# FFN, query and output projections of an attention + FFN block as four 32-column tiles

## The chip, the cores and the metric

The kernel runs on one core of a Trainium2 chip. The metric is the device time of one execution in microseconds (us); "before" is the median of three runs. A core has five engines that run their own instruction streams and wait for each other by semaphores: TensorE (PE; it multiplies, its weight loads are shown apart as PEld), VectorE (DVE), ScalarE (ACT), GpSimd (POOL) and SyncE (SP, which here issues most transfers). Products land in PSUM, eight banks of 128 partitions by 512 fp32 columns; everything else lies in SBUF.

## The reference

One block, attention with one shared key and value head beside an FFN, both on the same normalised input:

```python
xn = _layernorm(x)                       # x: 1 x 2048 x 640
# A: 32 query heads of 20 columns, one key head and one value head
q = (xn @ wq).reshape(B, S, 32, 20).transpose(0, 2, 1, 3)
k, v = xn @ wk, xn @ wv                  # 2048 x 20 each
scores = einsum("bhqd,bkd->bhqk", q, k) * 20 ** -0.5
o = einsum("bhqk,bkd->bhqd", softmax(scores), v)
A = o.transpose(0, 2, 1, 3).reshape(B, S, 640) @ wo
# B: FFN, 640 -> 1728 -> 640
Bf = silu(xn @ w1) @ w2
out = x + A + Bf
```

All inputs and the output are bf16.

## The kernel before

**Units and steps.** A unit is one head on one chunk of 512 queries: 32 heads by 4 chunks, 128 units. Three units form a group, and a group runs over 16 tiles of 128 keys, one *step* each: 43 groups, 688 steps. In a step `do_S` computes the scores of the group's units (L776): three matmuls of 32 rows by 128 columns, which stand in different row strips of the PE array and run together. Two sets of three PSUM banks (0 to 2, 3 to 5) take turns. ScalarE takes the exponential of two units at once (L794, 1,024 columns) into a ring E of `NBLK` blocks of 512 columns in SBUF. The third unit's exponential is worked out on VectorE (L808, L878) and GpSimd (L814) by integer arithmetic, in 637 of the 688 steps; in the others ScalarE takes three (1,536 columns).

**Sums with V.** `pv_mm` (L866) multiplies the exponentials by V: 128 rows by 32 columns. Each unit has a column strip of its own, so that three or four such matmuls run side by side, all into PSUM bank 6. After a group's last step VectorE copies the sums out, a transposing transfer turns them, GpSimd and VectorE divide by the sum of weights, and the result goes into o.

**Projections ("jobs").** A `Job` is a list of matmuls into one PSUM bank with a `consume` step after it. In the loop over steps all jobs share bank 7. `qd_job` makes queries (L1064, 5 matmuls of 512 columns, for 128 or, in one piece, 96 output columns of wq); `h_job` makes an FFN hidden tile (L1100, 5 of 512, then tanh on ScalarE L1113 and a product on VectorE L1118). The 14th hidden tile has 64 columns: `pair` puts two chunks of it into the two halves of one bank (L1103, 64-column tiles). `out_job` makes half an output row tile (320 columns): 14 FFN matmuls (L1168, the last on 64 rows only) or 5 of the output projection (L1173); `hold_job` (L1231, L1236) does this for the last rows and keeps the bank. All of these use the whole array, 128 by 128. So do the transposes (L1548), the key (L1567) and value (L1587) projections and the first query job (L1039) of the start.

**Order.** Nothing waits for a queue decision on the chip: `Sched` plays the program through with assumed durations and writes each engine's instructions in the resulting order. For PE, `step` chooses: scores first when they can start; else sums with V ("PV") or a job ("M"). It stays with the kind that PE is in (`pe_mode`), goes to PV under `press` (more than `NBLK - PV_PRESS` blocks of the ring waiting), and otherwise prefers PV if two are ready. `switch` adds `SWITCH` to the assumed duration when the kind changes. Jobs are taken from a queue in order, not before their `min_step`, which `fill_chunk` spreads over a chunk's steps; the last 16 steps prefer PV. Where PE has nothing to do, `fill` issues matmuls on zeros (L693, L699, L712) that change no result, if PE's recent share of work is low.

**The start.** x is loaded, statistics are taken, tiles are normalised into w2's space (`xa`), and transposed by PE or by transposing transfers (L1517). `late_loads` then loads w2 (L1353) and wo, and GpSimd doubles wo (L1539).

Of the kernel before, what the change touches and what calls it, by code (L numbers as in the profile page):

```python
# [14 lines left out]
P = 128  # L15
D = 640
H = 32
# [28 lines left out]
NBLK = 31  # L46
# [38 lines left out]
ACT_STATS = (4, 6, 9, 12, 14)  # L85
NW_ENG = ("dve", "dve", "dve")
# [258 lines left out]
class Job:  # L345
    def __init__(self, name, mms, reads, consume, gate=None, min_step=-1, banks=None, on_start=None, width=0, hold=None, use=None, n=1):
        self.name = name
        self.mms = mms
# [12 lines left out]
class Builder:  # L361
# [17 lines left out]
    def alloc(self):  # L379
# [4 lines left out]
        self.w2 = sb([P, FC, D], BF16)  # L384
# [186 lines left out]
    def step(self, now):  # L571
# [44 lines left out]
        if pv_n and (self.pe_mode == "PV" or press or self.pv_q[0].mode == "M"):  # L616
# [14 lines left out]
        if choice == "PV":  # L631
            head = self.pv_q[0]
            d = (0.216 if head.mode == "PV" else head.dur) + self.switch(head.mode)
        else:
            d = (job if job is not None else cand[0]).mms[0][0] + self.switch("M")
# [39 lines left out]
    def fill(self, now, until):  # L675
# [4 lines left out]
        onto = job is not None and job.begun and job.width > 0 and (self.pe_mode == "M" or not self.u_open)  # L680
        mode = "PV" if self.u_open and not onto else "M"
# [5 lines left out]
        if onto:  # L687
# [4 lines left out]
            def fn(pe):  # L692
                return pe.matmul(self.bk(b, 0, n), self.zero[:, 0:P], self.zero[:, 0:n], start=False, stop=False,  # L693
# [7 lines left out]
        else:  # L701
# [8 lines left out]

            def fn(pe):
                return pe.matmul(self.bk(b, 0, n), self.zero[:, 0:P], self.zero[:, 0:n], start=True, stop=True)  # L712
# [3 lines left out]
        op = sc.new("pe", n / 2400.0 + self.switch(mode), fn, [("zero",)], [ukey] if ukey else [],  # L716
# [16 lines left out]
    def do_mm(self, job, now, d):  # L733
# [6 lines left out]
        self.pe_mode = "M"  # L740
# [124 lines left out]
    def pv_mm(self, pe, q, w, kt, x, start, stop):  # L865
        return pe.matmul(self.bk(UBANK, 0, QW, q * SLOT, (q + 1) * SLOT), self.v[:, w, kt, :], x, start=start, stop=stop,  # L866
                         tile_position=(0, q * SLOT), skip_group_check=True)

# [188 lines left out]
    def qd_job(self, c, m, step=-1):  # L1057
# [4 lines left out]
        for k in range(DC):  # L1062
            def f(pe, b, k=k):
                return pe.matmul(self.bk(b, 0, QW, 0, rows), self.wq[:, k, lo:hi], self.xnT[:, k, c * QW:(c + 1) * QW],  # L1064
                                 start=(k == 0), stop=(k == DC - 1))
# [24 lines left out]
        return Job(f"q{c}_{m}", mms, reads, consume, min_step=step, width=QW if rows == P else 0)  # L1090

    def h_job(self, c, fk, step):
# [4 lines left out]
        for k in range(DC):  # L1097
            def f(pe, b, k=k):
                if not pair:
                    return pe.matmul(self.bk(b), self.w1[:, k, fk * P:(fk + 1) * P], self.xnT[:, k, c * QW:(c + 1) * QW],  # L1100
                                     start=(k == 0), stop=(k == DC - 1))
                for z in range(2):
# [577 lines left out]
```

## Time and profile before

| | |
|---|---|
| median of three runs | 734.33 us (733.43 to 734.65) |
| span of the profiled execution | 732.1 us |
| granted TensorE clock, mean | 0.997 |
| exponentials on ScalarE, L794 | 688 instructions, 661.9 us busy |
| scores on PE, L776 | 2,048 matmuls |
| sums with V on PE, L866 | 3,534 matmuls |
| projections on PE, L1064, L1100, L1168, L1173 | 95, 260, 448 and 144 matmuls |
| fills on PE, L693, L699, L712 | 5, 47 and 70 matmuls |

The span runs from the first to the last instruction of the profiled execution; a run's time holds some us more. A row of the profile gives line, engine, operation, tiles and shape, with the count behind an x; behind that come busy time and mean duration (ns) of one, and behind a further bar the idle time ahead of them with what ended it. In a timeline the first two numbers are start and length in us. A matmul's record lasts from its start until its results are out (about 0.38 us for 512 columns), and the next starts while it is still running; the distance of starts is what a piece costs the engine.

### The profile page before, as it was taken

The page shows a single profiled execution, that of the slowest core. Times are in us where ns is not written, and L with a number is a line of the kernel's source. Part 1 is how long each engine was busy: PE and PEld are TensorE (multiplying, and loading weights), DVE is VectorE, ACT ScalarE, POOL GpSimd, SP SyncE. Part 2 cuts the span into 40 slices and gives each one's busy share as a digit, 9 for nine tenths or more (in the row PEclk, how much of TensorE's full clock was granted, in tenths as well). Part 3 has the DMA queues.
Part 4 walks back from the last instruction along what each step waited for, and adds up shares of the span by engine and source line. Part 5 has one row for each costly group of instructions (what it writes and reads, how often), then busy time and mean ns, then how long its engine had stood idle before and what let it go on. Part 6 is the DMA issues. An engine that isn't in the chain of part 4 may idle for free.

```text
span 732.1 us, 18886 instructions
## 1 busy us (share of the span) xinstructions
PE 714.9 (98%) x6863; PEld 229.2 (31%) x6863; DVE 652.6 (89%) x1189; ACT 695.8 (95%) x780; POOL 524.8 (72%) x897
## 2 busy tenths in 40 slices
PE   8898999999999999999999999999999999999998
PEld 4432222223333233222333233222233322322335
DVE  7788898998998999999899999999989899999883
ACT  6999999999999999999999999999999999999960
POOL 4376877677787777777777777767778877776770
PEclk9999999999999999999999999999999999999999
DMA  9546000000003011000102011110002001200011
GB/s 273 148 123 190 15 17 17 21 15 17 23 9 44 9 52 52 21 18 17 9 8 52 9 26 46 40 19 23 14 8 45 9 9 34 62 9 8 9 38 37
DMA packets 58546, 29.22 MB, mean 40 GB/s; under 512 B 44406, under 2 KB 57814, under 8 KB 58454
## 3 DMA queue, kind: packets, MB, share of 16 engines
q1 hardware_dynamic: 56998, 27.79, 15.1%
q8 instruction: 56, 0.92, 0.6%
q10 hardware_dynamic: 1456, 0.22, 0.2%
q14 instruction: 36, 0.29, 0.1%
HBM read 11.44 MB, written 2.62 MB: 19 GB/s over the span
## 4 chain that ended last, share of the span: by engine, by line
PE 70%; ACT 20%; issue 5%; DVE 4%; DMA 1%; POOL 1%; DVEq 0%; ACTq 0%; POOLq 0%
PE psall L866 23%; PE psall L776 22%; ACT sbt L794 18%; PE psall L1168 8%; PE psall L1100 7%; PE psall L1173 2%; PE psall L1064 2%; PE psall L712 2%; ACT sbt L1113 1%; DVE sbt L808 1%; PE psall L699 1%; DMA sbt<-sbt 1%; DVE sbt L1118 1%; ACT sbt L1458 1%; DVE sbt L1438 0%
## 5 line engine op out<-in xcount | busy, mean ns | idle before, releaser
L794 ACT ACTIVATE sbt<-psall 128x1024 bf16<-128x1024 f32 (+2 forms) x688 | 661.9, 1110 | 9.2 <-PE psall L776 7.7
L814 POOL TENSOR_TENSOR sbt<-sbt 128x256 int32<-128x256 int32 x637 | 436.8, 692 | 158.6 <-DVE sbt L808 143.9
L808 DVE TENSOR_SCALAR sbt<-psall 128x512 int16<-128x512 f32 x637 | 425.9, 684 | 48.2 <-PE psall L776 43.3
L776 PE MATMUL psall<-sbt 32*128 32x512 bf16 x2048 | 269.6, 385 | 6.4 <-ACT sbt L794 3.3
L866 PE MATMUL psall<-sbt 128*32 128x512 bf16 x3534 | 269.2, 385 | 2.1 <-POOL sbt L814 2.1
L776 PEld LDWEIGHTS psall<-sbt 32*128 32x128 bf16 x2048 | 69.2, 91 | 246.8 <-ACT sbt L794 81.1
L878 DVE TENSOR_SCALAR sbt<-sbt 128x1536 int16<-128x1536 int16 (+1 forms) x218 | 132.0, 608 | 2.0
L866 PEld LDWEIGHTS psall<-sbt 128*32 128x32 bf16 x3534 | 66.8, 94 | 113.7 <-issue 77.6
L1168 PE MATMUL psall<-sbt 128*128 128x320 bf16 x448 | 85.4, 302 | 0.2 <-DVE sbt L1118 0.2
L1100 PE MATMUL psall<-sbt 128*128 128x512 bf16 x260 | 79.9, 384 | 2.2 <-DVE sbt L1118 1.9
L1168 PEld LDWEIGHTS psall<-sbt 128*128 128x128 bf16 x448 | 34.7, 97 | 43.7 <-issue 33.1
L1118 DVE SCALAR_TENSOR_TENSOR sbt<-sbt,psall 128x512 bf16<-128x512 bf16 x54 | 36.8, 682 | 2.3 <-ACT sbt L1113 0.7
L1113 ACT ACTIVATE sbt<-psall 128x512 bf16<-128x512 f32 x54 | 37.1, 687 | 0.0
L986 DVE CAST sbt<-psall 128x512 bf16<-128x512 f32 x43 | 29.3, 682 | 1.7 <-PE psall L866 1.6
L1100 PEld LDWEIGHTS psall<-sbt 128*128 128x128 bf16 x260 | 17.8, 97 | 40.7 <-issue 25.8
L1064 PE MATMUL psall<-sbt 128*128 128x512 bf16 (+1 forms) x95 | 29.2, 385 | 0.4 <-DVE sbt L1118 0.4
L1173 PE MATMUL psall<-sbt 128*128 128x320 bf16 x144 | 29.0, 303 | 0.5 <-issue 0.4
L972 POOL TENSOR_TENSOR sbt<-sbt 128x240 bf16<-128x240 f32 (+2 forms) x44 | 25.4, 578 | 2.3 <-DMA sbt<-sbt 1.4
L958 POOL TENSOR_TENSOR sbt<-sbt 128x44 f32<-128x44 f32 x84 | 26.0, 309 | 1.1
L956 POOL CAST sbt<-sbt 128x168 f32<-128x168 bf16 x42 | 14.1, 335 | 9.0 <-DMA sbt<-sbt 9.0
L712 PE MATMUL psall<-sbt 128*128 128x512 bf16 (+1 forms) x70 | 17.4, 403 | 1.9 <-POOL sbt L1368 1.5
L1185 DVE SCALAR_TENSOR_TENSOR sbt<-psall,sbt 128x320 bf16<-128x320 f32 x28 | 13.6, 486 | 6.1 <-PE psall L1168 5.9
(88 smaller groups left out, 207.9 us busy)
## 6 DMA issues: line engine op xcount, KB each, us to landing
sbt<-in_A_x_dram SPq DMA_DIRECT2D x32, 160.0 KB, 3.3
out_dram<-sbt SPq DMA_DIRECT2D x15, 160.0 KB, 1.8
sbt<-in_B_w_dram SPq DMA_DIRECT2D x5, 432.0 KB, 6.6
sbt<-sbt SPq DMA_DIRECT2D x105, 20.0 KB
sbt<-in_B_w_dram SPq DMA_DIRECT2D x13, 160.0 KB, 2.9
sbt<-sbt SPq DMA_TRANSPOSE x68, 2.4
sbt<-sbt SPq DMA_DIRECT2D x1, 1024.0 KB, 6.1
sbt<-in_A_wo_dram SPq DMA_DIRECT2D x5, 160.0 KB, 2.7
```

The lines of the kernel that those rows point to most:

```text
L776: ins = pe.matmul(self.bk(par3 + j), self.kT[r:r + SLOT, kk, kt * P:(kt + 1) * P], self.qT[r:r + SLOT, h // 4, (x // H) % 2, :], start=Tru ...
L794: return a.activation(self.E[:, b0 * QW:(b0 + na) * QW], self.ps[:, par3 * BANK:(par3 + na) * BANK], AF.Exp, scale=ACT_SCALE)
L808: return v.tensor_scalar(self.Z[:, zs, zp * QW:(zp + 1) * QW], self.bk(bb), 0.0, ZMAX, ALU.max, ALU.min)
L814: sc.new("pool", Y_TIME, lambda v: v.tensor_tensor(self.Y[:, zs, 1, zp * QW:(zp + 1) * QW].bitcast(I32), self.Z[:, zs, zp * QW:(zp + 1) * ...
L866: return pe.matmul(self.bk(UBANK, 0, QW, q * SLOT, (q + 1) * SLOT), self.v[:, w, kt, :], x, start=start, stop=stop, tile_position=(0, q * ...
L878: sc.new("dve", Y_SLOW + t_dve_4x(w), lambda v, k=k: v.tensor_scalar(self.Y[:, zs, k, 0:n * QW], Z, float(PH[k + 1][0]), None, ALU.add), z ...
L1064: return pe.matmul(self.bk(b, 0, QW, 0, rows), self.wq[:, k, lo:hi], self.xnT[:, k, c * QW:(c + 1) * QW], start=(k == 0), stop=(k == DC - 1))
L1100: return pe.matmul(self.bk(b), self.w1[:, k, fk * P:(fk + 1) * P], self.xnT[:, k, c * QW:(c + 1) * QW], start=(k == 0), stop=(k == DC - 1))
L1113: sc.new("act", t_act(QW), lambda a: a.activation(t, src, AF.Tanh, scale=0.5), [("B", b)], [("tb", tp)], prio=X_PRIO, name=f"th{c}_{fk}")
L1118: sc.new("dve", t_dve_ps(QW), lambda v: v.scalar_tensor_tensor(out=self.hT[0:rows, fk, :], in0=t, scalar=1.0, in1=src, op0=ALU.add, op1=AL ...
L1168: return pe.matmul(self.bk(b, 0, 320), self.hT[r0:r1, fk, i * P:(i + 1) * P], self.w2[r0:r1, fk, e0:e0 + 320], start=(m == 0), stop=(m == ...
L1173: return pe.matmul(self.bk(b, 0, 320), self.oT[:, k, i * P:(i + 1) * P], self.wo[:, k, e0:e0 + 320], start=(m == 0 and src != "ps"), stop= ...
```

## The change

The jobs of `qd_job`, `h_job`, `out_job` and `hold_job` issue each matmul as four (for 96 columns three) matmuls of 128 rows by 32 columns, side by side, as the sums with V do (`mm4`). Their `mode` is now "PV", so for the planner no change of kind lies between them and the sums with V; the first query job, keys, values and transposes keep "M". When such a job is ready and there is no `press`, `step` takes it ahead of the sums with V. The last FFN tile is used with all 128 rows: w2 gets a 15th slice, and GpSimd zeroes the 14th and 15th (after their last use as normalised x, before w2 is loaded), so that for each chunk the other half of the rows meets zero weights. For the space, the ring E has 30 blocks in place of 31. The fills at the start get shapes from a list, `WARM` (M: 128 by 128; T: four of 128 by 32; H: two of 128 by 64; S: three of 32 by 128; A: twelve of 32 by 32), and the first nine are assumed to last twice as long.

```diff
-NBLK = 31
+NBLK = 30
+WARM = "MMMMMMMMMMMMMAATTATMMAMSSASTMMHTHMMMM"
+COLD_FILLS = 9
...
-        self.w2 = sb([P, FC, D], BF16)
+        self.w2 = sb([P, FC + 1, D], BF16)
...
         choice = None
-        if pv_n and (self.pe_mode == "PV" or press or self.pv_q[0].mode == "M"):
+        jmode = None
+        if has_misc:
+            jmode = (job if job is not None else cand[0]).mode
+        if jmode == "PV" and not press and not (pv_n and self.pv_q[0].mode == "M"):
+            choice = "M"
+        elif pv_n and (self.pe_mode == "PV" or press or self.pv_q[0].mode == "M"):
             choice = "PV"
...
-            d = (job if job is not None else cand[0]).mms[0][0] + self.switch("M")
+            d = (job if job is not None else cand[0]).mms[0][0] + self.switch(jmode)
...
+            shape = WARM[self.nfill] if n == 512 and self.nfill < len(WARM) else "M"
+            if shape in "SA":
+                more = [("B", j) for j in range(3)]
+
             def fn(pe):
-                return pe.matmul(self.bk(b, 0, n), self.zero[:, 0:P], self.zero[:, 0:n], start=True, stop=True)
+                cols = {"M": P, "S": P, "A": SLOT, "T": SLOT, "H": 2 * SLOT}[shape]
+                for j in range(3 if shape in "SA" else 1):
+                    r = slice(j * SLOT, j * SLOT + SLOT) if shape in "SA" else slice(0, P)
+                    for a in range(0, P, cols):
+                        bb = j if shape in "SA" else b
+                        pos = dict(tile_position=(r.start, a), skip_group_check=True) if shape != "M" else {}
+                        ins = pe.matmul(self.bk(bb, 0, n, a, a + cols), self.zero[r, 0:cols], self.zero[r, 0:n],
+                                        start=True, stop=True, **pos)
+                return ins
...
-        op = sc.new("pe", n / 2400.0 + self.switch(mode), fn, [("zero",)], [ukey] if ukey else [],
+        d = n / (2400.0 if self.nfill >= COLD_FILLS else 1200.0)
+        op = sc.new("pe", d + self.switch(mode), fn, [("zero",)], ([ukey] if ukey else []) + more,
...
-        self.pe_mode = "M"
+        self.pe_mode = job.mode
...
+    def mm4(self, pe, b, lo, hi, lhsT, rhs, start, stop, rows=P):
+        ins = None
+        for r in range(0, rows, SLOT):
+            ins = pe.matmul(self.bk(b, lo, hi, r, r + SLOT), lhsT[:, r:r + SLOT], rhs, start=start, stop=stop,
+                            tile_position=(0, r), skip_group_check=True)
+        return ins
...
-                    return pe.matmul(self.bk(b), self.w1[:, k, fk * P:(fk + 1) * P], self.xnT[:, k, c * QW:(c + 1) * QW],
-                                     start=(k == 0), stop=(k == DC - 1))
+                    return self.mm4(pe, b, 0, QW, self.w1[:, k, fk * P:(fk + 1) * P],
+                                    self.xnT[:, k, c * QW:(c + 1) * QW], k == 0, k == DC - 1)
...
-                r0 = FLAST * (c % 2) if fk == FC - 1 else 0
-                r1 = r0 + FLAST if fk == FC - 1 else P
-
-                def f(pe, b, fk=fk, r0=r0, r1=r1, m=len(mms)):
-                    return pe.matmul(self.bk(b, 0, 320), self.hT[r0:r1, fk, i * P:(i + 1) * P],
-                                     self.w2[r0:r1, fk, e0:e0 + 320], start=(m == 0), stop=(m == tot - 1))
+                wk = FC if fk == FC - 1 and c % 2 else fk
+
+                def f(pe, b, fk=fk, wk=wk, m=len(mms)):
+                    return self.mm4(pe, b, 0, 320, self.hT[:, fk, i * P:(i + 1) * P],
+                                    self.w2[:, wk, e0:e0 + 320], m == 0, m == tot - 1)
...
-                return pe.matmul(self.bk(b, 0, 320), self.oT[:, k, i * P:(i + 1) * P],
-                                 self.wo[:, k, e0:e0 + 320], start=(m == 0 and src != "ps"), stop=(m == tot - 1))
+                return self.mm4(pe, b, 0, 320, self.oT[:, k, i * P:(i + 1) * P], self.wo[:, k, e0:e0 + 320],
+                                m == 0 and src != "ps", m == tot - 1)
...
-                w2p.append(lambda q, fk=fk, rows=rows, r0=r0: q.dma_start(self.w2[r0:r0 + rows, fk, :],
-                                                                          self.B_w2[fk * P:fk * P + rows, :]))
+                w2p.append(lambda q, fk=fk, rows=rows, r0=r0: q.dma_start(
+                    self.w2[r0:r0 + rows, fk + (r0 > 0), :], self.B_w2[fk * P:fk * P + rows, :]))
...
+        pool(0.9, lambda g: g.memset(self.w2[:, FC - 1:FC + 1, :], 0.0), [], [("xn", 12)], prio=2.0)
```

`qd_job`, `hold_job` and the two-chunk form of `h_job` change in the same way.

## The prediction

> **What bounds the kernel now.** I began with the head of the page: busy shares and the chain of work that ended last.
>
> ```profile
> span 732.1 us, 18886 instructions
> PE 714.9 (98%) x6863; PEld 229.2 (31%) x6863; DVE 652.6 (89%) x1189; ACT 695.8 (95%) x780; POOL 524.8 (72%) x897
> ...
> PE 70%; ACT 20%; issue 5%; DVE 4%; DMA 1%; POOL 1%; DVEq 0%; ACTq 0%; POOLq 0%
> ```
>
> TensorE is busy nearly always and carries 70% of the chain; ScalarE is close behind. The table of stretches shows where each sets the end.
>
> ```profile
> 280.00:360.00 80.00, 79.56 (x764) 23.94 (x756) 74.73 (x128) 79.72 (x90) 58.20 (x96) 1.00 0.10 22
> ...
> 710.00:720.00 10.00, 10.00 (x83) 5.67 (x82) 3.62 (x10) 0.07 (x1) 1.48 (x3) 1.00 0.01 2
> ```
>
> Columns: stretch, length, busy time of PE, PEld, DVE, ACT, POOL, clock, DMA. In the middle both PE and ACT look full; from 710 us ScalarE has nothing left and PE alone works. "Busy" hides something on both, as neighbouring instructions overlap, so I went on by start times. In the timeline of PE:
>
> ```profile
> 299.47 0.60 PE L1100 MATMUL psall<-sbt 128*128 128x512 bf16 x2
> 300.00 0.62 PE L866 MATMUL psall<-sbt 128*32 128x512 bf16 x8
> 300.55 0.39 PE L776 MATMUL psall<-sbt 32*128 32x512 bf16 x3
> ...
> 302.51 0.39 PE L1064 MATMUL psall<-sbt 128*128 128x512 bf16 x1
> 302.83 0.39 PE L776 MATMUL psall<-sbt 32*128 32x512 bf16 x3
> 303.15 0.61 PE L1064 MATMUL psall<-sbt 128*128 128x512 bf16 x2
> ```
>
> Three shapes of matmul take turns: scores (L776, 32 rows by 128 columns, three at once; S below), the sums with V (L866, 128 by 32, four at once; V) and the projections (128 by 128; M). Inside one shape a 512-column piece costs 0.216 us from start to start. From 302.51 to 302.83 one such piece takes 0.32, from 302.83 to 303.15 again 0.32: **each change of shape costs about 0.105 us**. From 299.47 two M pieces and the change to V take 0.53.
>
> I then summed start-to-start times of all PE groups between 80 and 710 us (630 us): 462 us stream columns, 131 us are changes into or out of S (1,266 of them), 9.4 us changes between V and M (92), 3.2 us changes to or from the 64-row shape of the last FFN tile, 4 us are fills, and about 20 us is the rest: some 10 ns extra on the first piece after a change, and waits. So PE has little to give, and what is taken from it counts.
>
> ScalarE, in the same way:
>
> ```profile
> L794 ACT ACTIVATE sbt<-psall 128x1024 bf16<-128x1024 f32 x625 | 594.5, 1090 | 4.9 <-PE psall L776 3.7 <-PE psall L866 0.4 <-ACT sbt L794 0.2
> ```
>
> One lasts 1090 ns, but starts come 904 ns apart in the median and 927 in the mean (584 of them between 80 and 700 us). Taking for each shape the pitch that 1 in 20 undercuts, ScalarE could do these 620 us in 605: **it would allow 14.7 us less**, and no more.
>
> **The change, part by part.**
>
> *Changes of shape that go.* M becomes V's shape: S still has both its neighbours, so none of the S changes goes. Over the whole trace I count 101 changes between V and M (55 M to V, 43 V to M, 3 from the odd query piece of 64 or 96 columns); two touch the V projection, which stays 128 wide, so 99 x 0.105 = 10.4 us go. The last FFN tile, padded to 128 rows, loses 40 changes (31 into it, 9 out of it to M or V) at 0.097 on average: 3.9 us. Some of each lies in the tail after 710 us (1.2 us together). Sum: -14.3.
>
> *What the new shape costs by itself.* A piece of four column tiles before S takes 321 ns, one M matmul 311; M ends a stretch before S 272 times: +2.7 us. S to V takes 321 against S to M 324, 326 times: -1.0. Net +1.7.
>
> *More instructions.* 260 + 90 + 592 + 24 M matmuls become four each, the odd pieces a few more: about 2,930 matmuls and as many weight loads added. Does a 320-column group still take 136 ns? The weight loads:
>
> ```profile
> L866 PEld LDWEIGHTS psall<-sbt 128*32 128x32 bf16 x3534 | 66.8, 94 | 113.7 <-issue 77.6 <-POOL sbt L814 5.6 <-DVE sbt L986 2.5
> L1168 PEld LDWEIGHTS psall<-sbt 128*128 128x128 bf16 x416 | 31.8, 97 | 35.5 <-issue 25.3 <-DVE sbt L1185 1.6 <-DVE sbt L1118 0.6
> ```
>
> A 32-column load lasts 94 ns, a 128-column one 97, and four small ones start within 6 ns, right behind the start of the group before: all are in after some 105 ns, under 136. Twice a V group follows a 288-column fill, by 122 and 130 ns, so its four loads needed no more. The V projection's matmuls of 20 columns start every 25 ns, twenty in a row: four pairs in 100 ns. The lower bound is thus 0. The upper one: groups of four have run in long bursts only at 216 ns; at that, 606 groups would cost 80 ns each, 48 us. The 122 ns is nearest to the case; I take 0.
>
> The Trainium skill speaks against this: "TensorE: Matmul & The Clock Gate", section "Part 3: Packing small matmuls — row/col tiling", lets weight loads overlap running matmuls only where the row group differs, and its section on LDWEIGHTS gives columns over 1.2 in ns, so about 107 ns for four loads of 32 columns, in the open in every group: by it some 100 us more for nearly a thousand groups (an estimate from that page). "TensorEngine Tiling (Array Packing)", section "Restrictions and Gotchas", adds that column tiling rules out the fast weight load. But all V groups here share their rows, their loads start under the running group, and they still follow at 216 ns, which is streaming alone. The measurement decides.
>
> *Order.* When a job is ready it now goes ahead of the sums with V unless more than 18 blocks wait (30 less 12; it was 19). M can be put beside V in any step for nothing, so steps can be filled with 136-ns pieces too; today a step of V alone averages 996 ns and one of M alone 915. Between nothing and about half of the 14.7 us that ScalarE allows could be won; against it, PE freed by 2% meets ScalarE more often, so part of the 14.3 can be lost as waiting. I set +0.5 for both together, from bounds of -7 and +6. One block less: with two blocks a step a round is 15 steps in 30 blocks as in 31, so 0.
>
> *The zeroing on GpSimd.* It waits for tile 12's transposing transfer (these are issued from 19.6 to 34 us) and fills 128 x 1280; the memset of 128 x 2560 took 2.23 us, so about 1.1. Behind it in GpSimd's queue are the additions (L814) that V matmuls wait for. Work waits on GpSimd only in spots (it is busy 15.5 of 20 us from 40 to 60), so it is mostly covered by idle time there: 0.2, bounds 0 and 1.1. The load of w2 into the zeroed tiles now waits for it, with all that is queued behind it on SP; but it is issued from 50.8 us (L1353), some 17 us after the last transposing transfer, so 0.
>
> *Start.* Fills run from 1.45 to 11.44 us, while the last normalisations they bridge begin at 9.86: counting nine fills at half clock makes the plan issue about nine fewer, up to -1.0. The new fills of mixed shapes have about a dozen changes at 0.105 in what is left: up to +1.2. I take 0, between -1.0 and +1.2.
>
> Sum: -14.3 + 1.7 + 0 + 0.5 + 0.2 + 0 = -11.9. The profiled execution has a span of 732.1; the runs' median is 734.33, so 2.2 us lie around it. 732.1 - 11.9 + 2.2 = **722.4**.
>
> **Rivals.**
>
> *Freed PE time is lost to ScalarE.* If the steps that lose a change of shape merely wait longer for the exponential, only the tail's 1.2 us remain against the 1.7 of the new shape: 734.3 - 1.2 + 1.7, about 735, or 731 if a third of the 14.3 gets through. For it: ScalarE's starts are at their floor in half of all steps. Against it: after 710 us PE alone works for 18 us, 65 of its matmuls there (L1168) being FFN work left over, so PE time saved earlier shortens this end.
>
> ```profile
> L1168 PE MATMUL psall<-sbt 128*128 128x320 bf16 (+1 forms) x65 | 10.2, 300 | 0.0
> ```
>
> *More than the changes of shape.* Jobs first and finer pieces let ScalarE run near its floor in the middle, and the left-over FFN work moves ahead of 710. Half of 14.7 with all of these 65 matmuls (65 x 0.136 + 1.0 = 9.8) is 17; the whole of both is 24.5: 710 to 717, say 714. For it: FFN jobs now go before V. Against it: PE must then find room for them in a middle that is full.
>
> *Slower: the groups of four don't follow at 136 ns.* If a 320-column group takes longer than 136 because of its loads or of issue, each ns costs 0.6 us over 606 groups; it decides from 11.9 / 606 = 20 ns, that is at 156 ns a group. At 160 the time is 737; at the 216 seen in V bursts, 771. Speaks for it that eight instructions per 136 ns for twelve microseconds (the tail) occur nowhere in this trace; against it the 122 ns and the 25 ns above.
>
> **How the numbers follow.** Forecast (718 to 728): 0.50. More: 0.20. Lost to ScalarE (728 to 735): 0.15. Slower by the groups of four, or as much by another way: 0.15. The likeliest case gives 722. Its own range is 716 to 729, the ends of the order and the start added to it; for 8 in 10 I go from 711, which keeps nearly all of the larger gain, to 736, which takes in all of the lost case. About 0.2% (1.5 us) is what can be told from no change. Faster 0.80 (forecast, more, and two thirds of lost), same 0.05, slower 0.15.
>
> **What would show it.** No idle of 0.1 us where V and projection matmuls meet; L1168 without a 64-row form; 320-column groups at 136 ns and their loads still under the group before; starts of 1024-column exponentials nearer to 904 than 927 in the mean; fewer than 65 L1168 groups after the last exponential. Wrong it would be if PE groups stretch, if exponentials wait for V matmuls that were put behind jobs, or if PE falls to half clock more often: it did so once here, for 3.4 us from 72.9 on, after a 2.1 us wait for GpSimd, and each such time costs 1.7 us.

## The result, and the profile after

The changed kernel takes 730.15 us (median of four runs, 729.25 to 731.11); the kernel before, beside it, 734.49. The ratio is 0.994 [0.9926, 0.9955]: 4.3 us are gained, where the prediction had 11.9 (the brackets are the 95% interval of the ratio). The head of the page of the kernel after:

```profile
span 728.6 us, 24857 instructions
PE 702.6 (96%) x9851; PEld 231.2 (32%) x9851; DVE 653.9 (90%) x1188; ACT 696.1 (96%) x780; POOL 528.6 (73%) x897
...
PE 68%; ACT 15%; DVE 9%; issue 6%; DMA 1%; POOL 1%; DVEq 0%; ACTq 0%; POOLq 0%
```

TensorE's busy time falls by 12 us, the span by only 3.5, and VectorE's share of the chain goes from 4% to 9%: something other than PE now ends more of the waits. In the timeline of PE and its weight loads (L801 scores, L891 sums with V, L897 all projections; other lines between are left out):

```profile
302.36 0.40 PE L897 MATMUL psall<-sbt 128*32 128x512 bf16 x4
302.38 0.10 PEld L891 LDWEIGHTS psall<-sbt 128*32 128x32 bf16 x4
302.59 0.39 PE L891 MATMUL psall<-sbt 128*32 128x512 bf16 x4
302.91 0.39 PE L801 MATMUL psall<-sbt 32*128 32x512 bf16 x3
```

A projection and a sum with V now start 0.23 us apart, close to the 0.216 of 512 columns alone, and the loads for the sum run while the projection does; only the change to the scores (0.32) is left. The instructions by shape:

```profile
L897 PEld LDWEIGHTS psall<-sbt 128*32 128x32 bf16 x3879 | 86.3, 95 | 87.0 <-issue 44.6 <-DVE sbt L1152 5.7 <-DVE sbt L833 4.1
...
L819 ACT ACTIVATE sbt<-psall 128x1024 bf16<-128x1024 f32 x626 | 593.2, 1088 | 12.1 <-PE psall L801 11.6
```

The small loads last 95 ns. Of the 353 groups of four 320-column matmuls that directly follow another one, half start within 136 ns of it and nine in ten within 147. And the table of stretches, with the columns of before:

```profile
280.00:360.00 80.00, 78.13 (x1102) 24.29 (x1099) 74.32 (x126) 79.72 (x90) 60.48 (x100) 1.00 0.08 19
...
710.00:720.00 10.00, 9.19 (x138) 4.08 (x134) 8.25 (x17) 4.86 (x8) 5.62 (x12) 1.00 0.20 15
```

In the middle ScalarE is as full as it was, while PE has gained idle time; from 710 us PE no longer works alone. The starts of the 688 steps' exponentials in the profiled executions say where the time went (us). From here on "the middle" is steps 52 to 687, and "the tail" runs from the start of the last exponential to the end of the last matmul:

| | to the first | steps 0–16 | 16–52 | 52–687 | tail |
|---|---|---|---|---|---|
| before | 16.86 | 26.17 | 38.69 | 627.33 | 19.66 |
| after | 17.62 | 28.22 | 41.70 | 628.84 | 8.80 |
| difference | +0.76 | +2.05 | +3.01 | +1.51 | −10.86 |

So the tail is 11 us shorter, the time up to step 52 is 5.8 longer, and the middle, which was to give most of the gain, gave none. I counted PE's time between the starts of its groups there: the streaming of columns, 0.105 us for a change of shape, and what is left, as waiting. Changes other than those of the scores fall from 12.4 us (123) to 0, waiting rises from 12.4 to 18.0, fills fall from 3.8 to 1.2, and the projections stream 157.1 us where it was 143.6: work that came out of the tail.

### The profile page after: what moved, and what is told of

Its sections match the earlier page's. It is cut to its first block, busy times and chain, and to the rows that moved or that the text cites. A ratio compares the mean times of both kernels' runs of the same rounds, so it can differ in the third digit from the quotient of the medians.

```text
span 728.6 us, 24857 instructions
## 1 busy us (share of the span) xinstructions
PE 702.6 (96%) x9851; PEld 231.2 (32%) x9851; DVE 653.9 (90%) x1188; ACT 696.1 (96%) x780; POOL 528.6 (73%) x897
## 4 chain that ended last, share of the span: by engine, by line
PE 68%; ACT 15%; DVE 9%; issue 6%; DMA 1%; POOL 1%; DVEq 0%; ACTq 0%; POOLq 0%
PE psall L891 24%; PE psall L801 22%; PE psall L897 19%; ACT sbt L819 13%; DVE sbt L833 4%; PE psall L734 2%; DMA sbt<-sbt 1%; DVE sbt L910 1%; DVE sbt L1018 1%; ACT sbt L1147 1%; PE psall L711 1%; POOL sbt L839 1%; ACT sbt L1491 1%; DVE sbt L1103 0%; DVE sbt L1152 0%
## 5 line engine op out<-in xcount | busy, mean ns | idle before, releaser
L819 ACT ACTIVATE sbt<-psall 128x1024 bf16<-128x1024 f32 (+1 forms) x688 | 661.0, 1108 | 15.5 <-PE psall L801 14.6
L839 POOL TENSOR_TENSOR sbt<-sbt 128x256 int32<-128x256 int32 x636 | 437.5, 693 | 157.5 <-DVE sbt L833 137.0
L891 PE MATMUL psall<-sbt 128*32 128x512 bf16 x3532 | 284.2, 386 | 7.2 <-POOL sbt L839 4.1
L801 PE MATMUL psall<-sbt 32*128 32x512 bf16 x2048 | 269.4, 385 | 10.9 <-ACT sbt L819 6.6
L897 PE MATMUL psall<-sbt 128*32 128x320 bf16 (+1 forms) x3879 | 241.5, 331 | 1.7 <-DVE sbt L1152 0.6
L801 PEld LDWEIGHTS psall<-sbt 32*128 32x128 bf16 x2048 | 68.6, 91 | 256.2 <-ACT sbt L819 97.9
L897 PEld LDWEIGHTS psall<-sbt 128*32 128x32 bf16 x3879 | 86.3, 95 | 87.0 <-issue 44.6
L891 PEld LDWEIGHTS psall<-sbt 128*32 128x32 bf16 x3532 | 71.3, 94 | 125.1 <-issue 90.3
L990 POOL TENSOR_TENSOR sbt<-sbt 128x44 f32<-128x44 f32 x84 | 27.6, 328 | 0.7
L988 POOL CAST sbt<-sbt 128x168 f32<-128x168 bf16 x42 | 13.6, 323 | 11.0 <-DMA sbt<-sbt 11.0
L734 PE MATMUL psall<-sbt 32*32 32x512 bf16 (+6 forms) x141 | 18.4, 400 | 1.9 <-POOL sbt L1401 1.5
L985 POOL TENSOR_TENSOR sbt<-sbt 128x84 f32<-128x84 bf16 x42 | 14.7, 349 | 0.0
L1611 POOL TENSOR_SCALAR sbt<-sbt 128x256 bf16<-128x256 bf16 x8 | 3.8, 477 | 14.9 <-DVE sbt L1609 14.8
L995 DVE RECIPROCAL sbt<-sbt 128x12 f32<-128x12 f32 x42 | 9.2, 219 | 6.0 <-POOL sbt L990 5.9
L1103 DVE TENSOR_SCALAR sbt<-psall 128x512 bf16<-128x512 f32 (+1 forms) x19 | 13.0, 684 | 1.3 <-PE psall L897 1.1
```

What stands on the lines that cost most here:

```text
L734: ins = pe.matmul(self.bk(bb, 0, n, a, a + cols), self.zero[r, 0:cols], self.zero[r, 0:n], start=True, stop=True, **pos)
L801: ins = pe.matmul(self.bk(par3 + j), self.kT[r:r + SLOT, kk, kt * P:(kt + 1) * P], self.qT[r:r + SLOT, h // 4, (x // H) % 2, :], start=Tru ...
L819: return a.activation(self.E[:, b0 * QW:(b0 + na) * QW], self.ps[:, par3 * BANK:(par3 + na) * BANK], AF.Exp, scale=ACT_SCALE)
L839: sc.new("pool", Y_TIME, lambda v: v.tensor_tensor(self.Y[:, zs, 1, zp * QW:(zp + 1) * QW].bitcast(I32), self.Z[:, zs, zp * QW:(zp + 1) * ...
L897: ins = pe.matmul(self.bk(b, lo, hi, r, r + SLOT), lhsT[:, r:r + SLOT], rhs, start=start, stop=stop, tile_position=(0, r), skip_group_chec ...
L990: pl.append((0.22, lambda v, lo=lo, hi=hi, i=i: v.tensor_tensor(w[:, :, 2, lo:hi], w[:, :, 2, lo:hi], ut[:, :, i, DH + 1:DH + 1 + hi - lo] ...
```

## The experiments

Each ratio is against the kernel before on the same chip, whose median was 733.5 to 733.8. The times by stage are from one profiled execution of each kernel.

**The tiles alone.** Three kernels are the kernel before with one edit each; order rules, kinds and fills stay as they were. `e_same`: the hidden, query and output projections' matmuls as four tiles; the FFN's 448 output matmuls (L1168) and their last tile stay whole.

```diff
-  return pe.matmul(self.bk(b), self.w1[...], self.xnT[...], ...)
+  return self.mm4(pe, b, 0, QW, self.w1[...], self.xnT[...], ...)
...
-  return pe.matmul(self.bk(b, 0, 320), self.oT[...], self.wo[...], ...)
+  return self.mm4(pe, b, 0, 320, self.oT[...], self.wo[...], ...)
```

> Edit: the kernel before, in which only the matmuls of the projections are issued as four 32-column tiles; the planner's kinds, order, fills and the 64-row last FFN tile stay, so every engine but PE has exactly the instructions of before, in the same order. Theory (PE time that is freed reaches the end when the order stays): 99 changes of shape at 0.105 us go (-10.4), the dearer end of a stretch ahead of the scores costs +1.7, so 725 to 727 us, about 8 us faster than before. Rival (ScalarE is the bound and takes the freed time as waiting): only the tail's 0.2 us between V and projections goes, 732 to 736 us. Rival (the four-tile groups are slower than one matmul): slower than before, over 736 us, with 320-column groups above 136 ns.

`e_tiles`: all projections, the padded tile and the zeroing too, which takes a ring of 30 blocks. `e_blk`: the ring alone.

```diff
-NBLK = 31
+NBLK = 30
```

> Before with every projection matmul as four 32-column tiles (the FFN's output matmuls too, which the kernel with the order of before left whole), the last FFN tile padded to 128 rows, w2's zeroing and a ring of 30 blocks; kinds, the rule of V first, and fills as before. Between steps 52 and 687 all 123 changes of shape other than those of the scores should go, 80 of which the earlier kernel had removed (8.1 us) without gaining. Theory (a change of shape in the middle lies beside a wait for ScalarE or VectorE to release banks): the further 43, 4.3 us, become waiting too: the middle stays between 626.5 and 628.5 us, its waits grow from 20 to 23 or 24 us, the time is 732 to 736 where before has 733.5. Only the tail, where PE works alone, gains, at most 1.2 us. Rival (the 64-row changes are not beside waits, and count one to one): the middle falls by 4, to 624, and the time is 729 or 730, which would make the padding alone worth the gain of the whole change.

> Before with a ring of 30 blocks in place of 31 and nothing else. Prediction: two blocks a step make 15 steps of either ring, so 0: 732.5 to 734.5 where before has 733.5. Rival: the shorter ring presses sums with V ahead of jobs more often (press begins at 18 waiting blocks, not 19), adding changes of shape between V and M at 0.105 us: with 20 or more of them the time rises by 2 us or more, to 735.5, and part of what the change lost would be the ring's.

| | time | ratio | changes of shape, 52–687 | waits, 52–687 | steps 52–687 | tail |
|---|---|---|---|---|---|---|
| before | 733.8 | | 12.4 | 12.4 | 627.3 | 19.7 |
| e_same | 735.41 | 1.0026 [1.0004, 1.0047] | 4.3 | 20.2 | 628.2 | 19.6 |
| e_blk | 735.95 | 1.0032 [1.0018, 1.0046] | 11.2 | 15.4 | 625.6 | 22.7 |
| e_tiles | 734.20 | 1.0003 [0.9991, 1.0015] | 0.6 | 24.9 | 626.3 | 21.3 |

`e_same` frees 8.1 us of PE time in the middle, and 7.8 of it come back as waiting; its whole time is no better than before's. `e_tiles` is best read beside `e_blk`, which has its ring and nearly its order: 10.6 us of changes go, 9.6 of waiting come, and the middle is 0.7 longer; the tail, where PE works alone, is 1.4 shorter. All the tiles and the padding are thus worth 1.75 us (735.95 − 734.20; the intervals of the two ratios don't overlap), of which the middle and the tail show 0.7; the rest would lie in the start, where `e_blk` was profiled with a stretch of half clock (below). That the 64-row tile's changes would count where the others don't is refuted as well.

Some 630 of the steps hold the same groups in the same order in `e_blk` and `e_tiles`. The 105 with such a change in them get 5.9 us shorter together, of the 11 that their 108 changes cost; the others get 6.8 longer. So about half of the freed time shows in the step itself, and other steps lose it again. Two steps show one way in which it goes. First `e_blk` (timeline):

```profile
212.76 0.39 PE L776 MATMUL psall<-sbt 32*128 32x512 bf16 x3
213.09 0.68 PE L1168 MATMUL psall<-sbt 128*128 128x320 bf16 x3
213.70 0.39 PE L776 MATMUL psall<-sbt 32*128 32x512 bf16 x3
213.81 0.49 DVE L1185 SCALAR_TENSOR_TENSOR sbt<-psall,sbt 128x320 bf16<-128x320 f32 x1
214.02 0.40 PE L866 MATMUL psall<-sbt 128*32 128x512 bf16 x4
214.36 0.31 PE L1168 MATMUL psall<-sbt 128*128 128x320 bf16 x1
214.60 0.39 PE L776 MATMUL psall<-sbt 32*128 32x512 bf16 x3
```

And the same two in `e_tiles` (L872 is the projection, L1193 the step that empties bank 7):

```profile
209.67 0.39 PE L776 MATMUL psall<-sbt 32*128 32x512 bf16 x3
209.99 0.59 PE L872 MATMUL psall<-sbt 128*32 128x320 bf16 x12
210.11 0.69 DVE L808 TENSOR_SCALAR sbt<-psall 128x512 int16<-128x512 f32 x1 [0.21 <-PE psall L776]
210.51 0.39 PE L776 MATMUL psall<-sbt 32*128 32x512 bf16 x3
210.71 0.48 DVE L1193 SCALAR_TENSOR_TENSOR sbt<-psall,sbt 128x320 bf16<-128x320 f32 x1
210.83 0.40 PE L866 MATMUL psall<-sbt 128*32 128x512 bf16 x4
211.25 0.32 PE L872 MATMUL psall<-sbt 128*32 128x320 bf16 x4
211.50 0.39 PE L776 MATMUL psall<-sbt 32*128 32x512 bf16 x3
```

The first step lasts 0.84 us instead of 0.94, since the change to the 64-row shape is gone. In the second the next projection starts 0.42 after the sum with V, not 0.22: there is no change to cover VectorE any more, which is emptying bank 7 until 211.19 (in `e_blk` until 214.30, and the projection starts at 214.36, when the change is done as well). From 212.76 to 214.60 it is 1.84 us, from 209.67 to 211.50 it is 1.83. VectorE is late because its work for the third unit (L808) came first. The same shift stands in the view of waits of PE's weight loads between 85 and 705 us, `e_blk` first (us, times, longest; the times that a release came last):

```profile
PEld psall L776 <- ACT sbt L794: 81.2, 220, 0.8
...
PEld psall L776 <- DVE sbt L808: 34.6, 86, 0.7
```

```profile
PEld psall L776 <- DVE sbt L808: 57.8, 148, 0.8
PEld psall L776 <- ACT sbt L794: 46.4, 120, 0.5
```

What the scores' banks wait for is ScalarE less often and VectorE more often.

The shorter ring costs 2.3 us by itself (1.3 to 3.4 by its interval), not by the mechanism of its rival: changes fall from 123 to 111, but 20 more groups of projections are left for the tail (140 against 120, 2.7 us). The tail is 3.0 us longer by that and the middle 1.7 shorter; the remaining 1.0 is not placed. The profiled execution also had half clock from 39.1 us on, after a wait of 1.63 us for VectorE, and steps 0–16 took 28.8 us in it; it lay 1.8 us above its median, and two of eleven executions show so low a mean clock (0.995), so I don't count that as the ring's.

**What PE waits for.** Four kernels shorten the other engines' work from step 64 on; the last 64 columns that each operation would write then keep older values. First ScalarE's exponentials, in the kernel before and in `e_same`:

```diff
+  z = 64 if t >= 64 else 0
-  return a.activation(self.E[:, b0 * QW:(b0 + na) * QW], self.ps[:, par3 * BANK:(par3 + na) * BANK], ...)
+  return a.activation(self.E[:, b0 * QW:(b0 + na) * QW - z], self.ps[:, par3 * BANK:(par3 + na) * BANK - z], ...)
```

> Edit: the kernel before, every instruction in its order, but from step 64 on each exponential on ScalarE covers 64 columns fewer (960 of 1,024; the last 64 keep older values, so the sums are not the reference's). This takes about 53 ns a step, 33 us in all, from ScalarE and nothing from PE. Theory (ScalarE paces the middle and PE, with about 615 us of its own work between steps 52 and 687, is the next bound): 722 to 727 us, the middle falls from 627 to 615 to 620 us. Rival (PE already paces the middle): within 2 us of the kernel before.

> Edit: the run with the order of before and four-tile projections, with the same shorter exponentials. Theory (the 8 us of freed changes of shape are real on PE and were hidden by ScalarE alone): 714 to 720 us, 6 to 8 us faster than the kernel before with the shorter exponentials. Rival (they are hidden by something else: VectorE's release of the third bank, or the fixed order): within 2 us of that kernel.

Then VectorE's first operation on the third unit (L808) as well:

> Edit: the kernel before with the order unchanged and, from step 64 on, ScalarE's exponentials and VectorE's step on the third unit's scores (its first operation on them) both 64 columns shorter, so that all three banks of scores come free 53 to 67 ns earlier (the last 64 columns keep older values). Theory (the scores' banks pace the middle; with both shorter, PE is what is left): the middle falls under the 620.7 us of the run with ScalarE alone shortened, to 612 to 618, about 720 to 725 us. Rival (waits for the projections' one bank, or the fixed order, hold it): no further gain, 727 to 728 us.

> Edit: the order of before with four-tile projections and the same two shortenings. Theory (the freed changes of shape show once ScalarE and VectorE are out of the way): 6 to 8 us faster than the kernel before with the same shortenings. Rival (a change of shape ahead of a job lies beside the wait for the projections' bank, which VectorE empties, and costs nothing there, whatever ScalarE does): no more than 3 us faster.

| steps 52–687 (us) | before's shape | four tiles as in e_same | difference | freed |
|---|---|---|---|---|
| nothing shortened | 627.33 | 628.16 | +0.8 | 8.1 |
| ScalarE shorter | 620.70 | 620.09 | −0.6 | 8.1 |
| ScalarE and VectorE shorter | 619.61 | 615.01 | −4.6 | 8.1 |

The whole times were 727.93 (0.9922 [0.9908, 0.9936]) and 725.50 (0.989 [0.9874, 0.9906]), then 727.66 (0.9905 [0.9888, 0.9922]) and 722.73 (0.985 [0.9832, 0.9869]). In the middle of the profiled executions the tiles still bring nearly nothing with ScalarE alone made faster (0.6 us); with both, 4.6 of the 8.1 us come through. In the whole times the tiles lose 1.7 with nothing shortened and bring 2.4 with ScalarE shorter and 4.9 with both, so ScalarE alone may let more through than the one profile shows. Neither case reaches the 6 to 8 us expected, and in before's shape VectorE's shorter step brings nothing clear of noise (727.93 to 727.66), as its rival had it. The tiles' time was thus hidden behind ScalarE and VectorE together. Of the last 3.5 us, 2.5 are still waiting: 7.4 us of waits in the last kernel, 4.4 of them ahead of projections, for their one bank, where the kernel beside it has 4.9. The changes to and from the scores cost some 1.2 us more there.

**The order.** `e_vfirst` is the kernel after with the old rule: sums with V first.

```diff
-        if jmode == "PV" and not press and not (pv_n and self.pv_q[0].mode == "M"):
-            choice = "M"
-        elif pv_n and (self.pe_mode == "PV" or press or self.pv_q[0].mode == "M"):
+        if pv_n and (self.pe_mode == "PV" or press or self.pv_q[0].mode == "M"):
```

> Edit: the changed kernel with the old rule of choice: sums with V ahead of jobs when PE is in their kind, which jobs now share. Theory (taking jobs first uses them up, and at the end of a group, while VectorE copies the sums' bank, PE has nothing to run and the scores come late): waits of PE between steps 52 and 687 fall from 18 us to about 12; FFN work comes back into the tail, a few us; 724 to 728 us, 2 to 6 us faster than the changed kernel's 730. Rival (the waits come from ScalarE and not from the choice): 729 to 731 us, waits still near 18 us.

`e_first_before` is the kernel before with only the new rule, for the same jobs, the shapes as they were:

```diff
+        nj = (job if job is not None else cand[0]) if has_misc else None
+        first = nj is not None and (nj.name[0] in "hFG" or ("wqd", 0) in nj.reads)
+        if first and not press and not (pv_n and self.pv_q[0].mode == "M"):
+            choice = "M"
-        if pv_n and (self.pe_mode == "PV" or press or self.pv_q[0].mode == "M"):
+        elif pv_n and (self.pe_mode == "PV" or press or self.pv_q[0].mode == "M"):
```

> Edit: the kernel before with only the rule of order of the change (a ready FFN, query or output job goes ahead of the sums with V unless blocks press), matmuls untouched. Theory (the rule pays only where it costs no change of shape; here each step that mixes them pays 0.105 us or more, and what ScalarE and VectorE do not hide ends in the tail): 738 to 750 us. Rival (the rule alone, by moving FFN work ahead of the last exponential, is the gain and the tiles are not needed): 724 to 731 us.

`e_vfirst` takes 745.88 (1.0166 [1.0147, 1.0186]), far from what I expected: as jobs and sums are now of one kind, the rule that keeps the kind keeps the sums whenever one is ready, projections starve (137.4 us of them in the middle, not 157.1, and 19.4 us of fills, not 1.2), and the tail is 29.4 us. In it, from 709.6 us on:

```profile
L895 PE MATMUL psall<-sbt 128*32 128x320 bf16 (+1 forms) x684 | 26.3, 304 | 0.5 <-DVE sbt L1150 0.5
```

That is 160 groups of 320 columns and 11 of 512, where the kernel after has 34 groups of 320 in its tail, FFN and output projection together (the line is that of the helper):

```profile
L897 PE MATMUL psall<-sbt 128*32 128x320 bf16 x136 | 6.0, 300 | 0.5 <-DVE sbt L1184 0.5
```

In the kernel before, beside the 65 FFN matmuls of 320 columns (L1168), 48 of the output projection stand there:

```profile
L1173 PE MATMUL psall<-sbt 128*128 128x320 bf16 x24 | 3.7, 300 | 0.0
L1236 PE MATMUL psall<-sbt 128*128 128x320 bf16 x16 | 2.8, 299 | 0.0
L1231 PE MATMUL psall<-sbt 128*128 128x320 bf16 x8 | 1.7, 299 | 0.0
```

So 113 pieces became 34; 79 x 0.136 is 10.7 us, nearly all of the 10.9 by which the tail is shorter.

`e_first_before` takes 751.60 (1.0241 [1.0221, 1.0261]): 279 changes of shape in the middle instead of 123, a tail of 33.8. Tiles without the rule are worth nothing (734.2), the rule without tiles loses 18 us; together, with the kinds merged and the new fills, they make 730.15. (Tiles with the new rule and separate kinds were not run.) With tiles a projection can be put beside a sum with V without a change of shape, and PE's waits are filled with work out of the tail: from `e_tiles` to the kernel after the middle streams 16.3 us more of projections and is only 2.5 longer, as 7.0 of waits, 2.6 of fills and 2.8 of sums with V are gone there, and the tail is 12.5 shorter.

**The start.** In the kernel after, GpSimd waits, and PE with it (timeline; L975 is the transposing transfer, L988 GpSimd's first step on its data, L839 the third unit's last step):

```profile
71.84 0.33 POOL L988 CAST sbt<-sbt 128x168 f32<-128x168 bf16 x1 [5.38 <-DMA sbt<-sbt]
...
73.89 0.40 PE L891 MATMUL psall<-sbt 128*32 128x512 bf16 x4 [3.46 <-POOL sbt L839]
...
74.30 0.61 PE L801 MATMUL psall<-sbt 32*128 32x512 bf16 x3
```

The transfer's data land 5.6 us after it was issued, where the median of these transfers is 2.5. Three loads stand ahead of it in SP's queue (w2, wo, a fill of a query tile from an SBUF buffer; the view of SP's queue):

```profile
54.57 7.33 SPq L1386 DMA_DIRECT2D sbt<-in_B_w_dram  x15
61.94 3.39 SPq L1569 DMA_DIRECT2D sbt<-in_A_wo_dram  x5
65.38 0.70 SPq L1562 DMA_DIRECT2D sbt<-sbt  x1
66.12 2.13 SPq L975 DMA_TRANSPOSE sbt<-sbt  x1
```

GpSimd stands for 5.4 us, PE for 3.5, and then PE's clock is halved for 6.8 (scores at 0.61 us). The kernel before has the same loads in the same order, and its transfer lands after 6.2 us:

```profile
50.78 8.50 SPq L1353 DMA_DIRECT2D sbt<-in_B_w_dram  x15
59.33 2.48 SPq L1536 DMA_DIRECT2D sbt<-in_A_wo_dram  x5
61.85 0.70 SPq L1529 DMA_DIRECT2D sbt<-sbt  x1
62.60 2.12 SPq L943 DMA_TRANSPOSE sbt<-sbt  x1
```

There GpSimd stands for 3.3 us, PE for 2.06, and the half clock lasts 3.4:

```profile
72.44 0.40 PE L866 MATMUL psall<-sbt 128*32 128x512 bf16 x4 [2.06 <-POOL sbt L814]
```

So the change did not reorder the queue; it came to this place 3.5 us later, and its wait was longer. Why longer is not shown. The first FFN tanh writes the buffer that the query fill reads, and so has to come behind it: it starts at 82.55 us, at 74.47 in the kernel before. The fill had landed by 71.0, so the stall and the slow clock have their share in that. `e_start` takes the new fills away, `e_late` moves the late transfers apart (its fill copies a buffer already written anew, so the second half's queries are others):

```diff
-WARM = "MMMMMMMMMMMMAATTATMMAMSSASTMMHTHMMMM"
-COLD_FILLS = 9
+WARM = ""
+COLD_FILLS = 0
```

> Edit: the changed kernel with all fills at the start of the 128 by 128 shape and none counted double, as before. Theory (the changes of shape among the fills delay the first exponential by 0.76 us against before): first exponential back at 16.9 us, 729 to 730 us, 0.5 to 1 us faster than the changed kernel. Rival (the order behind it is decided anew, and a key matmul is placed well or badly by it): first exponential 0.8 us earlier, but the time anywhere between -4 and +4 us of 730, decided at the step 12 to 16.

> Edit: the changed kernel in which wo is loaded (and doubled) after the second group and the zeroing transfer of the second query half after the third, and no longer right behind w2 after the first. Theory (the second group's transposing transfer lies behind these loads, GpSimd waits 5.4 us for it with the additions that V needs behind, PE idles 3.5 us and then runs at half clock for 6.8 us): the transfer lands 3 us or more earlier, no or one window of half clock, 723 to 727 us, 3 to 7 us faster than the changed kernel. Rival (w2's own 2.2 MB are what it waits for): the wait stays over 4 us and the time within 1 us of 730.

`e_start` has 729.57 (0.9939 [0.9919, 0.9959]), the same as the kernel after: steps 0–16 gain 1.0, 16–52 gain 2.6, but a half-clock stretch comes at 54.9 instead, the middle takes 1.8 more, and the first exponential starts at 18.04, later still. Its executions differ: 726.33 and 728.16 us at a mean clock of 0.998, 730.30 to 730.59 at 0.992 or 0.993. `e_late` has 722.21 (0.9847 [0.983, 0.9863]), with full clock throughout.

`e_order` does the latter rightly, in the kernel after; `e_order_before` does it in the kernel before; `e_order_start` is `e_order` with the edit of `e_start`.

```diff
+        if g == LATE_G + 1:
+            self.late_wo(("U", up))
...
         def late_loads(key):
+            qz(1, [key])
             load_w2([key])
+
+        def late_wo(key):
             load_w("sp", "o", ...
...
-            qz(1, [key])
```

> Edit: the changed kernel with the transfer that fills the second half of the query tiles issued ahead of w2's load, and not behind w2 and wo, and with wo loaded and doubled after the second group. Theory (that transfer reads the buffer that the first FFN tile's tanh needs, so no FFN work can start before it is done, PE has only V and fills from 45 to 80 us, the second group's transposing transfer is late behind the loads, and PE falls to half clock): FFN matmuls start 15 to 25 us earlier, no half clock after the start, 721 to 725 us. Rival (only the stall of 3.5 us counts): 726 to 728 us.

> Edit: the same two moves in the kernel before. Theory (the start's loss is common to both kernels, only larger by 3 us in the changed one): 727 to 731 us, a smaller gain than in the changed kernel. Rival (the loss belongs to the change): 733 to 735 us.

> Edit: the run with the reordered loads on the changed kernel (722 us), with all fills at the start 128 by 128 and none counted double. Theory (counting fills double moved the last key matmul behind V work and cost about 2 us in steps 0 to 16, and the shapes of the fills matter for nothing): steps 0 to 16 take 26 to 27.3 us in place of 28.2, 720 to 721 us. Rival: no change, 721.5 to 722.5 us.

| | time | ratio | 0–16 | 16–52 | 52–687 | tail |
|---|---|---|---|---|---|---|
| e_order_before | 727.86 | 0.9921 [0.9908, 0.9935] | 26.16 | 36.24 | 627.38 | 14.82 |
| e_order | 721.93 | 0.9845 [0.983, 0.986] | 28.19 | 37.65 | 624.72 | 8.59 |
| e_order_start | 723.25 | 0.9853 [0.9839, 0.9867] | 26.19 | 39.01 | 626.21 | 8.55 |

Stretch 45 to 80 us of the kernel after, then of `e_order`:

```profile
45.00:80.00 35.00, 30.21 (x299) 8.38 (x300) 26.76 (x49) 29.66 (x33) 24.30 (x41) 0.92 0.44 130
```

```profile
45.00:80.00 35.00, 32.50 (x389) 9.34 (x393) 31.80 (x57) 34.79 (x39) 26.98 (x45) 1.00 0.47 133
```

ScalarE works 34.8 of 35 us, not 29.7, at full clock, and the first FFN tanh starts at 62.07 us. `e_order` is the best version, 7 to 8 us under the kernel after (7.0 by the ratios, 8.2 by the medians) and 11.5 under before. The kernel before gains from the same two moves, so with them in both kernels the change is worth 727.86 − 721.93 = 5.9 us: half of the 11.9 forecast. The tail gives 6.2 and the middle 2.7; steps 0–16 and 16–52 cost 2.0 and 1.4. Steps 0–16 take 28.2 to 28.5 us in the four kernels with the new fills (after, `e_vfirst`, `e_late`, `e_order`); without these fills they are at 27.2 (`e_start`) and 26.19 (`e_order_start`), and 26.17 before. In the kernel after, the last key matmul (L1601) stands behind 25 sums with V, and the scores come after it:

```profile
40.53 1.69 PE L891 MATMUL psall<-sbt 128*32 128x512 bf16 x25
42.15 0.28 PE L1601 MATMUL psall<-sbt 128*128 128x256 bf16 x1
...
43.58 0.61 PE L801 MATMUL psall<-sbt 32*128 32x512 bf16 x6 [0.45 <-POOL sbt L1611]
```

So the fills shift the plan; whether by their shapes or by the doubled durations, and whether the key matmul is all of the 1 to 2 us, no run separates. That the time gained nothing when they were taken out (723.25, 721.93) goes with a stretch of half clock from 55 us on in `e_order_start`.

## Why the prediction was right or wrong

**Changes of shape that go: the step that failed.** −14.3 was counted one to one, because "PE has little to give, and what is taken from it counts". The price per change was right and all the changes went. But in the middle PE's 98% hid that the steps also wait for VectorE and ScalarE to release banks: `e_tiles` against `e_blk` frees 10.6 us there, 9.6 come back as waiting, and the middle gets 0.7 longer. Only the share in the tail came (1.2 forecast, 1.4 measured). The rival "Freed PE time is lost to ScalarE" describes the middle, and 730.15 lies in its range (728 to 735, given 0.15); with one correction: it is both engines, and the short pitch of ScalarE (904 ns) is reached no more often than before. The mean pitch, named as a sign of success, is 926 ns where it was 927, and what ScalarE lost above its floor between 80 and 700 us went from 14.7 to 13.5 us only.

**Order: mis-sized, outside its bounds.** Taken at +0.5 between −7 and +6. Against `e_tiles`, which has the tiles with before's rule and kinds, the kernel after is 2.5 us longer in the middle and 12.5 shorter in the tail: −10.0 for the rule and the merged kinds together. (The −15.7 between `e_vfirst` and the kernel after is the rule's worth where the kinds are merged already and the old rule starves the projections.) It is what made the gain, not by a faster middle but by moving projections out of the tail. The rival "More" had that part, though for the 65 FFN pieces alone: of 113 pieces of 320 columns after the last exponential 34 are left.

**Start: mis-sized.** Between −1.0 and +1.2, it was +5.8 by step 52. Of this, 0.8 up to the first exponential goes with the moment at which that execution got its full clock (last section), and is no cost of the change. 2.0 in steps 0–16 come with the new fills and the plan behind them. Of the 3.0 in 16–52, 1.6 go when the late transfers are moved in both kernels (4.0 gained in the kernel after, 2.5 in before); 1.4 stay, and no run says why. The prediction named half clock as a danger at 1.7 us each; here it lasted 3.4 us longer than before, behind a wait 1.4 longer, and two of the four executions of the kernel after show a higher mean clock (0.997, not 0.995) and are 1.2 us faster. I priced what fills cost, and neither what they do to the plan behind them nor the transfers that stand ahead of one that GpSimd waits for, in both kernels.

**Ring block: 0 forecast, +2.3 measured** in before's order.

**Right:** groups of four follow at 136 ns, so the rival with a slow group is out, and the rule of the Trainium skill weighed there with it: in "TensorE: Matmul & The Clock Gate", "Part 3: Packing small matmuls — row/col tiling", weight loads overlap only where row groups differ; the 3,879 matmuls here share their rows, a load for four of this shape starts under the running projection (302.38 us above), and the groups still follow at 136 ns. The measurement decides. A group of four before the scores takes 321 to 322 ns, and the scores before one 321, as taken for +1.7. The zeroing took 1.16 us on GpSimd, between two waits of 1.9 and 2.2 us, for a transfer and for VectorE, and so delayed nothing there. Two slips in the sums change little: there are 616 groups of 320 columns, not 606, and the ends of the order and the start added to 722.4 give 714 to 729, not 716 to 729.

The total lies within the 711 to 736 given for 8 in 10 by luck, as three errors met: against the terms of the sum the middle gave 12.4 us too little and the start cost 5.8 too much, while the tail gave 9.7 more. It lies outside the likeliest case's own 716 to 729, and the gain is little over a third of the 11.9 forecast.

**Left open:** why the clock is granted between 4.1 and 7.4 us after the start in runs of nearly one program; the padding apart from the tiles, which no run had by itself; whether a longer ring would help the kernel after; what makes the shorter one leave 20 groups to the tail; and the 3.5 us of the tiles that stay hidden with both engines shortened.

## What to carry to other kernels

On an engine that is nearly always busy, ask of each saved piece what else ends at the same place: where a bank's release by two other engines lies beside it, little comes of it until both are faster too. Freed time is then worth what can be moved into it, so look for work that waits alone at the end and for the rule that lets it forward. And when a change makes a planner shift, read the first steps anew: which transfers stand ahead of one that an engine waits for, and when the plan now comes to them.

## What the runs showed of the hardware

The first exponential follows the moment at which PE's full clock begins: full clock from 4.4 us gave it at 16.7, from 5.7 at 17.4, from 6.5 at 17.7, from 7.4 at 18.1, all with before's fills. The kernel after fits in between, with 6.0 and 17.6, so the number and shape of the fills don't show. With before's fills the moment lies anywhere between 4.1 and 7.4 us, and moves the first exponential from 16.5 to 18.2.

After a wait of 2.06 us (before) the clock was halved for 3.41 us, after one of 3.46 us (after) for 6.83, twice as long. The length of a wait alone does not decide: half clock followed a wait of 1.69 us in `e_blk` (until 74.9 us), and none followed one of 1.73 us in `e_vfirst` (until 75.6). In each trace the changes of clock lie whole multiples of 3.413 us apart (from 4.63 to 72.90 us it is 20 of them in the kernel before), so where a wait falls between them may matter too; no run varies that alone. The Trainium skill's "TensorE: Matmul & The Clock Gate", "Part 1: The HAM clock gate (the "warmup" mystery)", gives a free-running window of 3.4 us by which the clock is judged; one and two windows agree with both rows. Its condition for a drop, an idle window of about 3.4 us, is stricter than what the kernel before shows with 2.06 us.
